# Products of zeros on TensorE ahead of the first useful work, with a newly searched order of all engines

## The chip, the cores and the metric

The kernel runs on one core of one Trainium2 chip. The metric is the device time of one execution in microseconds (us); lower is better. Most executions of a kernel agree within half a percent, so the differences here (0.3 to 1.2%) need several executions each. Two single executions fell in a slow state (311.9 us at a granted clock of 0.951, and 308.81 us); they are left out of the ratios.

A ratio is the mean time of one kernel's fast executions over that of the kernel before, in the same rounds on the same chip. It comes with a 95% interval, and it is not quite the ratio of the medians quoted beside it.

Engine names: PE is TensorE, PEld its weight loads, DVE is VectorE, ACT is ScalarE, POOL is GpSimd, SP is SyncE.

## The reference

Sliding-window attention with a linear bias, followed by a two-layer network whose activation is h·cos(h).

```python
B, H, S, D = 8, 8, 576, 64; window = 128; d_ff = 2048
scores = q @ k.T / sqrt(D) + bias, only where 0 <= row - col < window
attn   = softmax(scores) @ v
x = attn.transpose(0, 2, 1, 3).reshape(4608, 512)
h = x @ w_in                      # 512 -> 2048
out = (h * cos(h)) @ w_out        # 2048 -> 512
```

## The kernel before

The program is a list of operations with their reads and writes. A packed table (`STARTS`) gives each a place on a common time line, in units of 25 ns. The operations are sorted by it and each engine's queue is filled in that order. Waits are derived from the reads and writes. So the table changes only the order; how long a wait lasts is decided on the chip.

```python
def load_v(b, order=range(NBLK)):
    for t in order:
        op("pool", [lambda e, ...: e.dma_start(vp[b % 2][0:rows, t, :, 0:64], v[b, ...])],
           r=[("vinit", b % 2)], w=[("v", b % 2, t)], dma=f"ldv{b % 2}{t}", ...)

def constants():
    for i in range(2):
        op("dve", lambda e, i=i: e.memset(vp[i][:, :, :, 64:65], 1.0), w=[("vinit", i)])
        op("dve", lambda e, i=i: e.memset(vp[i][64:128, 4, :, 0:64], 0.0), w=[("vinit", i)])
        op("dve", lambda e, i=i: e.memset(Pt[i][:, 1024:1088], 0.0), w=[("Pt", i)])
    # ... cos bias, tails of the key tiles

load_first_q()                    # SP issues it, ACT and DVE cast it
load_qk("k", k, 0, 0)             # POOL from here: first keys
distances(); identity()           # POOL computes
load_qk("q", q, 0, 1); load_qk("k", k, 0, 1)
constants()
load_v(0, range(2))               # waits for the clearing of vp[0] on DVE
load_w_in(0); load_v(0, range(2, NBLK))
masks()
for n in range(2):
    qk_transposes(0, "q", n, 0, OB); qk_transposes(0, "k", n, 0, UB)
for u in range(1, 4): load_w_in(u)
load_qk("q", q, 1); load_qk("k", k, 1)
for u in range(4): load_w_out(u)
load_v(1)
```

After that come scores, exponentials, masks, products with V, and nine stages of the network; the network's first stage (stage 0) starts while attention of the first batch still runs.

The softmax here doesn't subtract the row's maximum and nothing guards it: scores larger than these inputs give would overflow.

Of the kernel before, what the change touches and what calls it, by code (L numbers as in the profile page):

```python
# [14 lines left out]
B, H, S, D = 8, 8, 576, 64  # L15
# [12 lines left out]


STARTS = (  # L30
    "c-oy-4RjM#7S8lXpQEnNCmz~Ifbcpkbr@<5Lz`xjG@)q-w5Ao0r7czF)LKhHt!yi7Es9Wf6}niJgZv#9q#}wUi@TMj3cD+N2"
    "+E&|g1D>fuIs@cJm61hX`1YvN!q4O6)`=Xd2@f>y!+kn-a7^^6f%T=K`s<bi0_I^=m|f9JZRv8unb%D+4cVtxOl_40Y&&094"
    "rWF*HF}Ba9|_t-fQ5rzc|B%{%wQ(tI%c3hSOfY?{Id#15t!}An;IBm|9eQ&wWvbxDXeG$sk?i*QH$oyn*95U8}jA8wxVK_@{"
    "qxmheu|GOl+>O7vXz?-tN(2BkF^wT`{&S}xkgzzqNp90Eq@N8n8C)^G6vt~300u7?|P@EDE-hYI3*FKNOJm2im{hDs7HM!m1"
    "Me;-a?bB5mGA^1^%Vr>S;6v=uhwhjh!Vi0uNEe<qsfoR{54q6b3=7K>lUhbmdvQfO^;w4QYZ6MldD2j1cbjP3=ib2s3V`GTH"
    "Y_QD`R)n~SasZ_SL$_XGA&pMjNqV9nijV6GFT#F_ojPFgL9Q$OKJHQ_H4GX*!(=F6kfFd(8`L>Wk^;lXdiysCL~Z!vc9+r`e"
    ")7H1r|zrY_`m?%iGe`4#x)h{>WjXQl3Ztk<`C?H#-s5%aQS8ZGw_YHkLX?y!{SIx!xOSk!u=#6dt**KY+37d8|*LGctd|f(c"
    "6zsNG<|UTyHRHhq&IZNa6PU0+I!OLE*;o;L5J3m|`*eg@wz-;sn7PdLqPuf(-V1T@0JX1uh?hxZX>~#|4My${=EP$7~-QJPu"
    "$k2V*!9g$FlyzQzs$PM^9LhrIXaOu0*^Id+#}B%Lt_48(jA#IAc|zz7XHE&D=@?Wn<iNq-aJf<sOj8YXeU{+1c(-uk(M!^9a"
    "J2A|@Qp#*DMnki|F_1*t;W$^d6j(Bdo*X#6pjc3f8HYQaDM^tcUE4WARAOGFF8<U+*r_}}*(0jcHOUpm(k@9AgdGo971-?C%"  # L40
    "6Gl&_*SPaaUvTHsaoLVN`0g=n6Goc;JF4(tj!QU>r;Xk>t3ZDBKDA>(HZCLwWzp!b`G{WiCfl0&o(=Pen9<Y9VOGea48&K@D"
    "MExIi^L}td_^%&vv_j<ePyt~M(lCePso%IL`jlzLY5Gvh#2ixBOVhZV48Cs+aV&J%0}fCq*7arK-bw1$_N}ZyYq-gNI*84GZ"
    "Q=oDk9Uf<9VbaB1%ch9M}U<ej!y}q?pJxh!)#NEkF2y<GQ7HzrXI*FZ`<GkbhCLd&Y`vLesk!?w?Ur>0fkLebb4_!f{eW-=;"
    "N9?M0|4mwYZ?PvdAw>FKrp{Cv_WTs`4DwF*ytU6w<H6oUq0!%_cyRn=DcC)yrY7cv18R_boULWz}N!EByV!U!qEguqD{(UdP"
    "!2O}zBq|`!W8fPgqFJ>8T2a(zwYls&UFZtft1%^y{1{|0&u2jfsQ5LYLWu{zML-y{shdyi~nf7G_%O2NE8J9|~CrM2;%Uwj6"
    "Y634o^CCXk0gw@rUiO{9h&1slLPVxKAz_lP<e`>NjjfBvPLd0R_bUAd=yKXIkrWB+k@i3M7i5!M#^mWYXDZo5NgbWOqWI=)A"
    "~XcGFn3rg)fX&VGcDE(xx3P*C4%p}B%R~Us2)ju5|VsAN>AaQgjeh93`ji>S>kERW~}L(31JeCjXWBE+i5T%ni)aHT0uhpbG"
    "6I0mar^C;?d*AY5zC^_?eW)WDTGYX(TQ7j;vjnw=ZgGBIT}GE6Yzim5(W5Q<Pr=h_$&-K?aW4*J2-G%Dvcu9m>chgrzGhJg`"
    "sx9e&YhvM;M+lF2^OC%Dt>d8;fbMkk$o8`~qz6ptAHE?QFdSC>CH73!eD_}Bcq%?r<dct<Yq#brE3{jz%1@>{bthEM~Q%+n{"
    "+hv@U!vM?UsM3Q%jmS;;^<vS;We#??$pLl=k{nK(@U90YGtFdNoJACq@k4lvGAw|!bkx<NZzz_gRlJ`Mb^g)Vv#+ypZ;nAuK"  # L50
    "jJj&<cA|S9m(s#^lRA7FUIIZD9`ezgg^Io?=LvOc7`iQ*iD2Jn1VX0Uw-XJ;7cjvs%6-JdHYl%Ed7M?s6Axi0Q+f#l?PGvby"
    "8QrHI+ahEEHKv!<^g#kki6ZVr|01SU~I~No+V(Gn_L1CSKd0ywVzjwo`kdTc}Awl)5ob_+~(}6&abLm+<sF=^XsXOshxR5_~"
    "BPl*6$kUooTq2ypi<0sa~|q?i6V1L_*1h`cp05T5r8^xB7bPy7%^5pS$MX0mg-CmyQG`F#Xv`t%OhBt^-AM$~d&9VV*}3U!y"
    "-0{gQkS?Pn<x8kuv}$Zx{WP*s2$zpXYUg%CF+!a{7o)?&H7?&0h%JrjsGDX$O;O%3x?lovHO@My_ds(NKP4Fv?{=BkyXnb>?"
    "u%Ew@Xrz0Ti9A4CtB%1A8i0**Xa}(h-$cZUat|Ov{U{JdrW;zS_H06&3l1K?MDepj|)XvJ3?UctV{4?b(QpcdYWtRII^jX*s"
    "nOu2z<qyZ8$r>#y*6o$O*H+EWeZ0<Dwm(qof4BJUQ|q%wh}YAxB*hH~(?h%FW&@qqx9&aXJ>@Mt{t-}Ro~8BJv=#@F5taGyJ"
    "9+vIT-yPdKE#u|2jNf281rInVTs75^C<Z@k#+S$RxL9b<IV<jHUsaFM4eK_wz5StAYW(?ox*!hQ&pu$Ms=KHL^dfC1aqlLaZ"
    "#hQCFjv<Qa?u7{Ph_!U%9<Fy%stfCM8hBl*p3($+kwk*gjFxnn8+clTAhI7m}0a&96e2W3EIG7ECjz)xp~S8kPX%vUQfpg?Q"
    "#Ib!(ba-Fr4X(*C!arE@D@wrp7}%hP+RE4SZ-dx~?Cg!u18%k|f6YJV^XD*T<&E5y<TZ>0MhG(tXh?nG7GvDMa>Hr?>@R%+A"
    "RT7-vVcvLKfnFrEB>CUMUl(f!eWRy=j?HuTByvC*Ed-Ti^B<hBhwf8(#AK@WFww;-n?7U@eg-?e*!{;PyrHs5&*A{A%Bu6Vp"  # L60
    "(cVk7!Yyd+I_b$h>~tUhOu1ELPWII@m^iYsMV};36iaxu{V*1=nA-rwD!5#vq@+r@McXGY9{^>p&`u4fS)~}TEZFEBpINYMN"
    "_*9_RcD&oH@Cl8Mh>k}zI;wt=J`DgztlIsU2~Vksy1g2E=5Ecl8jV~pTQ^x!K9;lc<@JgC^?w-d-el3z*ydaq)jl-`LW&5q!"
    "{53QK>{iRfsQ|GXi-QW{D2$19qu4pwrA<!g3;J^1kIZW1-YeguI*tN)EBS8yRu7%$e)JewNd*fryp%KR2~NbxdL&=`Q8KN!7"
    "-bJ67%Rn3R7rI$yF+v&lZDoR>VZ=k~wg`I1Tb0LvSk4L1<E(W<O(q^nHIldD8WtzuPQ%KXMMZ}mrFO9FgllwyGba|KpaCon`"
    "EAfl3wPywZOBcJv?Vv~3(QrUxOrqAOL>l}niZeE7Yjz_K40>soqeE>lT&x&%~G~BUxF$+Kt(6}6r1MorG6x2zCr{)xY+vsai"
    "CYF4^gf+aisu_m+`y1qAyBdn{ZuPVESE?1nWPir!-&?NayG>-HGMl=0o0J|u{j%cI2N>Hp|E(=0OXfp!*@{*7qSRBX#q<aEw"
    "UOOf_RVAmq<NlNv-`AVx9KQMUjb6)$#Nj=5MN7saTePIRQ*KSSquf<G@JF<njmZS=%1S~<W~E}_?%To`s+5?h>Z}+zida<CP"
    "^wqG>$dD4H-urDatcRS_d{V$3{rI7THy)XH(K3WC^0)3DIhuIF$NB>i+?MBOA>"
)


# [150 lines left out]
def bass_alibi_sliding__then__act_gcu_kernel(  # L222
# [8 lines left out]
    with ExitStack() as ctx:  # L231
# [3 lines left out]
        R = Plan(nc, ctx)  # L235
        op = R.op
# [165 lines left out]
        def tail_zero(b):  # L402
# [3 lines left out]
                    :, 4, :, 64:128], 0.0), w=[("tr", "k", b % 2), ("ktail", b % 2)], occ=250,  # L406
               lat=300)

        def masks():
            for h in range(H):  # L410
                op("act", lambda e, h=h: e.activation(
                    EM[:, h, :], dif[:, :, :].rearrange("p a b -> p (a b)"),
                    ACTF.Exp, scale=slopes[h]), r=["dif"], w=[("EM", h)], occ=306, lat=400,
                   table=0)


        def qk_transposes(b, which, n, part, banks):

            t0, R, groups = PIECES[b][n]
            jj = groups[2 * part:2 * part + 2]  # L420
            c0 = 64 * (t0 // 32)

            def dst(i):
                return ps[:, banks[i], :].bitcast(BF16)[:, 0:128 * (jj[i][1] - jj[i][0])]

            def f(e):
                ins = None
                for i, (j0, j1) in enumerate(jj):
                    for j in range(j0, j1):
# [34 lines left out]
        def scores(us, slot):  # L464
# [577 lines left out]
```

## Time and profile before

| | before |
|---|---|
| median of three executions | 308.57 us |
| span of the profiled one | 306.7 us |
| PE busy | 293.7 us, 96% |
| first work on PE | 5.64 us |
| PE at half speed, by the spacing of its products | 5.64 to 21.44 us |

Busy time and the chain of waits, from the page of the kernel before. The first line is busy time, share of the span and number of instructions of each engine; the second is the chain of waits by engine.

```profile
PE 293.7 (96%) x2881; PEld 198.9 (65%) x2900; DVE 253.0 (82%) x540; ACT 204.6 (67%) x294; POOL 95.2 (31%) x122
PE 93%; DVE 3%; DMA 1%; issue 1%; ACT 1%; ACTq 0%
```

Everything here points at PE. But a matmul's recorded length can be longer than the distance to the next one: at 21.1 us the products of 65 columns are recorded at 0.25 us each and start 0.055 us apart. So an engine can read as 100% busy (PE here 2.98 of the 2.98 us from 18.39 to 21.37 us) while the products stand further apart than they need to.

PE's timeline of the kernel before, in the opening. Columns: start, length of the group, engine and line, operation, output<-inputs, shape, count, and in brackets the idle time before it and what ended it.

```profile
5.64 1.06 PE L431 MATMUL ps<-ident,qrows 128*64 128x128 bf16 x16 [5.64 <-ACT qrows L321]
8.85 0.82 PE L484 MATMUL ps<-qt,kt 64*128 64x256 bf16 x8 [1.29 <-DVE kt L398]
13.69 0.33 PE L569 MATMUL ps<-vp,p 128*128 128x65 bf16 x3 [0.73 <-issue]
18.39 0.42 PE L738 MATMUL ps<-xT,w_inb 128*128 128x256 bf16 x1
19.50 1.67 PE L738 MATMUL ps<-xT,w_inb 128*128 128x256 bf16 x7
23.13 1.26 PE L738 MATMUL ps<-xT,w_inb 128*128 128x256 bf16 x10
26.88 4.20 PE L738 MATMUL ps<-xT,w_inb 128*128 128x256 bf16 x37
```

Seven products take 1.67 us at 19.5 us, 37 take 4.20 us at 26.9 us; in the chain of waits they are 0.23 us and 0.109 us apart. The products of 65 columns stand 0.054 us apart up to 21.4 us and 0.031 us after it. So in this trace the array runs at about half speed at first. The clock record in the trace has its first entry, 1.00, at 21.44 us. Views that print the granted clock assume 1.00 ahead of the first entry (they print 1.00 for 5.64 to 13.69 us and for 13.69 to 21.44 us), and so hide the slow opening, 15.8 us here.

### The profile page before, as it was taken

Reading aid. Unit: us, or ns where it says so; the run is one execution under the profiler, and the core shown is the slowest. Engines: PE = TensorE matmul, PEld = TensorE weight load, DVE = VectorE, ACT = ScalarE, POOL = GpSimd, SP = SyncE. Lnnn points to the kernel's source line nnn. Section 1 sums busy time; section 2 is a strip of 40 time slices with the busy share of each in tenths; the row PEclk is TensorE's granted clock in tenths of the full one; section 3 lists DMA queues with packets and bytes.
Section 4 is the critical chain, followed back from the end, with each engine's and each line's share of the span. In section 5 each row is a group of like instructions: output and inputs, shape, how many; then the busy total and the mean of one; then the engine's idle time right before and its main releaser. Section 6 shows DMA issues by size and latency. Waiting matters only on the chain.

```text
span 306.7 us, 7126 instructions
## 1 busy us (share of the span) xinstructions
PE 293.7 (96%) x2881; PEld 198.9 (65%) x2900; DVE 253.0 (82%) x540; ACT 204.6 (67%) x294; POOL 95.2 (31%) x122
## 2 busy tenths in 40 slices
PE   2799999999999999999999999999999999999995
PEld 2568845545875578546788887468745765566784
DVE  1678885979978998889998998798999976795983
ACT  5796777688585776788765875678747846545311
POOL 5999240007997801770169004000000000000000
PEclk9999999999999999999999999999999999999999
DMA  7999999959999999999699988673033022020223
GB/s 144 142 192 211 207 173 183 111 96 182 176 156 172 158 156 180 164 165 175 100 168 134 191 122 62 113 141 100 18 98 79 0 84 63 2 68 0 71 87 122
DMA packets 148353, 38.09 MB, mean 124 GB/s; under 512 B 133984, under 2 KB 147040, under 8 KB 148320
## 3 DMA queue, kind: packets, MB, share of 16 engines
q0 software_dynamic: 99344, 18.10, 75.0%
q1 hardware_dynamic: 48976, 19.54, 31.2%
q8 instruction: 23, 0.38, 0.5%
q14 instruction: 10, 0.08, 0.1%
HBM read 36.70 MB, written 9.44 MB: 150 GB/s over the span
## 4 chain that ended last, share of the span: by engine, by line
PE 93%; DVE 3%; DMA 1%; issue 1%; ACT 1%; ACTq 0%
PE ps L714 35%; PE ps L855 33%; PE ps L484 5%; PE ps L738 5%; PE ps L799 5%; PE ps L569 3%; PE ps L431 2%; PE ps L572 2%; DMA ob<-in_q_dram 1%; PE ps L676 1%; PE ps L475 1%; PE ps L558 1%; PE ps L556 1%; DVE xnat L610 1%; DVE gT L724 0%
## 5 line engine op out<-in xcount | busy, mean ns | idle before, releaser
L714 PE MATMUL ps<-xT,w_inb 128*128 128x512 bf16 (+1 forms) x557 | 126.2, 355 | 0.9 <-ACT p L514 0.4
L720 ACT ACTIVATE cos<-ps,halfpi 128x512 f32<-128x512 f32 x128 | 82.5, 687 | 47.8 <-PE ps L714 33.8
L724 DVE TENSOR_TENSOR gT<-ps,cos 128x512 f16<-128x512 f32 x128 | 83.1, 686 | 15.6 <-ACT cos L720 14.9
L714 PEld LDWEIGHTS ps<-xT,w_inb 128*128 128x128 bf16 x576 | 54.4, 98 | 44.2 <-DVE gT L724 5.5
L514 ACT ACTIVATE p<-ps 128x768 bf16<-128x768 f32 (+1 forms) x64 | 56.1, 915 | 13.8 <-PE ps L484 9.8
L328 POOL DMA_DIRECT2D vp<-in_v_dram x40 | 33.9, 873 | 65.8 <-PE ps L572 34.5
L538 DVE TENSOR_TENSOR p<-p,emask 128x512 bf16<-128x512 bf16 (+2 forms) x96 | 42.2, 460 | 5.3 <-ACT p L514 5.0
L855 PE MATMUL ps<-wsum,gT 128*128 128x256 f16 x256 | 46.0, 273 | 0.3 <-issue 0.2
L855 PE MATMUL ps<-wsum,gsum 128*128 128x256 f16 x256 | 45.6, 273 | 0.0
L855 PE MATMUL ps<-w_outb,gT 128*128 128x256 f16 x256 | 43.4, 273 | 0.2
L338 POOL DMA_DIRECT2D qnat<-in_q_dram x30 | 25.4, 885 | 24.0 <-DMA qt<-qnat 22.1
L855 PEld LDWEIGHTS ps<-w_outb,gT 128*128 128x128 f16 x256 | 24.8, 98 | 7.0 <-DVE ob L879 0.4
L855 PEld LDWEIGHTS ps<-wsum,gT 128*128 128x128 f16 x256 | 23.8, 98 | 6.3 <-issue 0.3
L855 PEld LDWEIGHTS ps<-wsum,gsum 128*128 128x128 f16 x256 | 23.9, 98 | 6.1 <-issue 0.6
L855 PE MATMUL ps<-w_outb,gsum 128*128 128x256 f16 x128 | 27.6, 273 | 0.2
L338 POOL DMA_DIRECT2D knat<-in_k_dram x30 | 25.5, 906 | 3.8 <-DMA kt<-knat 2.2
L610 DVE TENSOR_TENSOR xnat<-ps,rec 128x256 bf16<-128x256 f32 x56 | 22.2, 418 | 1.0 <-DVE rec L608 0.2
L484 PE MATMUL ps<-qt,kt 64*128 64x128 bf16 (+1 forms) x320 | 20.1, 252 | 1.4 <-DVE kt L398 1.3
L569 PEld LDWEIGHTS ps<-vp,p 128*128 128x128 bf16 x256 | 16.1, 100 | 6.0 <-issue 3.1
L569 PE MATMUL ps<-vp,p 128*128 128x65 bf16 x256 | 19.0, 197 | 0.9 <-issue 0.7
L484 PEld LDWEIGHTS ps<-qt,kt 64*128 64x128 bf16 x320 | 11.7, 98 | 9.6 <-issue 3.8
L572 PE MATMUL ps<-vp,p 128*128 128x65 bf16 x192 | 17.7, 196 | 0.0
(76 smaller groups left out, 335.2 us busy)
## 6 DMA issues: line engine op xcount, KB each, us to landing
out_dram<-ob SPq DMA_DIRECT2D x32, 256.0 KB, 2.7
vp<-in_v_dram POOLq DMA_DIRECT2D x32, 128.0 KB, 7.1
qnat<-in_q_dram POOLq DMA_DIRECT2D x24, 128.0 KB, 8.5
knat<-in_k_dram POOLq DMA_DIRECT2D x24, 128.0 KB, 12.7
w_inb<-in_moe_w_in_dram POOLq DMA_DIRECT2D x4, 512.0 KB, 9.5
w_outb<-in_moe_w_out_dram POOLq DMA_DIRECT2D x4, 512.0 KB, 21.3
out_dram<-ob SPq DMA_DIRECT2D x8, 128.0 KB, 1.8
qrows<-in_q_dram POOLq DMA_DIRECT2D x1, 576.0 KB, 14.7
```

The source lines that it names most:

```text
L328: op("pool", [lambda e, t=t, rows=rows: e.dma_start(vp[b % 2][0:rows, t, :, 0:64], v[b, :, 128 * t:128 * t + rows, :].rearrange("h p d -> ...
L338: fns.append(lambda e, t=t, rows=rows: e.dma_start(nat[which][b % 2][0:rows, t, :, :], src[b, :, 128 * t:128 * t + rows, :].rearrange("h p ...
L484: ins = e.matmul(ps[:, banks[x], c0:c1], keys_ap(b, x, pr, kc), query_ap(b, x, pr, qb, 128 * nb), start=True, stop=True)
L514: op("act", lambda e: e.activation(P[i][:, :, 0:hi], src_[:, :, 0:hi], ACTF.Exp, scale=0.125), w=held + [("P", i)], occ=920 if G else 691, ...
L538: op("dve", lambda e, p=p, m=m: e.tensor_tensor(p, p, m, ALU.mult), r=[("P", i), ("EM", h0), ("EM", h1)], w=[("P", i)] if n != 1 else [("P ...
L569: ins = e.matmul(o, P[i][:, x, d0:d0 + 128], V[:, kc, h, 0:65], start=True, stop=not two)
L572: ins = e.matmul(o, P[i][:, x, p0:p0 + 128], V[:, kc - 1, h, 0:65], start=False, stop=True)
L610: op("dve", lambda e: e.tensor_tensor(o, U[:, :, :, 0:64], rv[:, :, :, None].broadcast_to([128, 2, 2, 64]), ALU.mult), r=[("rec", n % 2)], ...
L714: op("pe", lambda e, kc=kc, c0=c0: e.matmul(ps[:, bank, c0:c0 + n], w_in[:, kc, 128 * fc:128 * fc + 128], xT[:, kc, (r0 + c0) % XR:(r0 + c ...
L720: op("act", lambda e: e.activation(cosb[ci][:, :], ps[:, bank, :], ACTF.Sin, bias=halfpi[:, 0:1]), r=["halfpi"], w=[("B", bank), ("cos", c ...
L724: op("dve", lambda e: e.tensor_tensor(gT[gi][:, fc, :], ps[:, bank, :], cosb[ci][:, :], ALU.mult), r=[("cos", ci)], w=[("B", bank), ("g", ...
L855: op("pe", lambda e, t=t, fc=fc, bk=bk: e.matmul(ps[:, bk, 256 * t:256 * t + 256], lhs(fc, t), rhs(fc), start=first and fc == 0 and (last ...
```

## The change

The intent: in the trace above TensorE is at half speed until 21.44 us, and it idles while the first queries load (until 5.64 us). I expected it to speed up sooner if it is kept busy; no trace had shown that by then. So it is given products of zeros to do, nine of 512 columns at the start and two of 384 before the first scores. Then the order of all engines was searched again.

```diff
 STARTS = (
-    ... the old order, packed
+    ... the new order, packed (every engine's order differs)
 )
+        def warm(count, n, key):
+            if key == "warm":
+                op("dve", lambda e: e.memset(P[NP - 1][:, 0, :], 0.0), w=[("P", NP - 1)], ...)
+            for _ in range(count):
+                op("pe", lambda e: e.matmul(ps[:, SB[3], 0:n], P[NP - 1][:, 0, 0:128],
+                                            P[NP - 1][:, 0, 0:n], start=True, stop=True),
+                   r=[("P", NP - 1)] + (["kfirst"] if key == "warm2" else []),
+                   w=[("B", SB[3]), key], ...)
...
         load_first_q()
+        warm(9, 512, "warm")
         load_qk("k", k, 0, 0)
...
             qk_transposes(0, "k", n, 0, UB)
+            if n == 0:
+                warm(2, 384, "warm2")
```

(Three more lines make the first transposes and the first scores follow the zeros.)

More of the change, by code (lines that the diff above doesn't have):

```diff
@@ L30 @@
 STARTS = (
-    "c-oy-4RjM#7S8lXpQEnNCmz~Ifbcpkbr@<5Lz`xjG@)q-w5Ao0r7czF)LKhHt!yi7Es9Wf6}niJgZv#9q#}wUi@TMj3cD+N2"
-    "+E&|g1D>fuIs@cJm61hX`1YvN!q4O6)`=Xd2@f>y!+kn-a7^^6f%T=K`s<bi0_I^=m|f9JZRv8unb%D+4cVtxOl_40Y&&094"
-    "rWF*HF}Ba9|_t-fQ5rzc|B%{%wQ(tI%c3hSOfY?{Id#15t!}An;IBm|9eQ&wWvbxDXeG$sk?i*QH$oyn*95U8}jA8wxVK_@{"
-    "qxmheu|GOl+>O7vXz?-tN(2BkF^wT`{&S}xkgzzqNp90Eq@N8n8C)^G6vt~300u7?|P@EDE-hYI3*FKNOJm2im{hDs7HM!m1"
-    "Me;-a?bB5mGA^1^%Vr>S;6v=uhwhjh!Vi0uNEe<qsfoR{54q6b3=7K>lUhbmdvQfO^;w4QYZ6MldD2j1cbjP3=ib2s3V`GTH"
@@ L36 @@
-    "Y_QD`R)n~SasZ_SL$_XGA&pMjNqV9nijV6GFT#F_ojPFgL9Q$OKJHQ_H4GX*!(=F6kfFd(8`L>Wk^;lXdiysCL~Z!vc9+r`e"
-    ")7H1r|zrY_`m?%iGe`4#x)h{>WjXQl3Ztk<`C?H#-s5%aQS8ZGw_YHkLX?y!{SIx!xOSk!u=#6dt**KY+37d8|*LGctd|f(c"
-    "6zsNG<|UTyHRHhq&IZNa6PU0+I!OLE*;o;L5J3m|`*eg@wz-;sn7PdLqPuf(-V1T@0JX1uh?hxZX>~#|4My${=EP$7~-QJPu"
-    "$k2V*!9g$FlyzQzs$PM^9LhrIXaOu0*^Id+#}B%Lt_48(jA#IAc|zz7XHE&D=@?Wn<iNq-aJf<sOj8YXeU{+1c(-uk(M!^9a"
-    "J2A|@Qp#*DMnki|F_1*t;W$^d6j(Bdo*X#6pjc3f8HYQaDM^tcUE4WARAOGFF8<U+*r_}}*(0jcHOUpm(k@9AgdGo971-?C%"
@@ L41 @@
-    "6Gl&_*SPaaUvTHsaoLVN`0g=n6Goc;JF4(tj!QU>r;Xk>t3ZDBKDA>(HZCLwWzp!b`G{WiCfl0&o(=Pen9<Y9VOGea48&K@D"
-    "MExIi^L}td_^%&vv_j<ePyt~M(lCePso%IL`jlzLY5Gvh#2ixBOVhZV48Cs+aV&J%0}fCq*7arK-bw1$_N}ZyYq-gNI*84GZ"
-    "Q=oDk9Uf<9VbaB1%ch9M}U<ej!y}q?pJxh!)#NEkF2y<GQ7HzrXI*FZ`<GkbhCLd&Y`vLesk!?w?Ur>0fkLebb4_!f{eW-=;"
-    "N9?M0|4mwYZ?PvdAw>FKrp{Cv_WTs`4DwF*ytU6w<H6oUq0!%_cyRn=DcC)yrY7cv18R_boULWz}N!EByV!U!qEguqD{(UdP"
-    "!2O}zBq|`!W8fPgqFJ>8T2a(zwYls&UFZtft1%^y{1{|0&u2jfsQ5LYLWu{zML-y{shdyi~nf7G_%O2NE8J9|~CrM2;%Uwj6"
@@ L46 @@
-    "Y634o^CCXk0gw@rUiO{9h&1slLPVxKAz_lP<e`>NjjfBvPLd0R_bUAd=yKXIkrWB+k@i3M7i5!M#^mWYXDZo5NgbWOqWI=)A"
-    "~XcGFn3rg)fX&VGcDE(xx3P*C4%p}B%R~Us2)ju5|VsAN>AaQgjeh93`ji>S>kERW~}L(31JeCjXWBE+i5T%ni)aHT0uhpbG"
-    "6I0mar^C;?d*AY5zC^_?eW)WDTGYX(TQ7j;vjnw=ZgGBIT}GE6Yzim5(W5Q<Pr=h_$&-K?aW4*J2-G%Dvcu9m>chgrzGhJg`"
-    "sx9e&YhvM;M+lF2^OC%Dt>d8;fbMkk$o8`~qz6ptAHE?QFdSC>CH73!eD_}Bcq%?r<dct<Yq#brE3{jz%1@>{bthEM~Q%+n{"
-    "+hv@U!vM?UsM3Q%jmS;;^<vS;We#??$pLl=k{nK(@U90YGtFdNoJACq@k4lvGAw|!bkx<NZzz_gRlJ`Mb^g)Vv#+ypZ;nAuK"
@@ L51 @@
-    "jJj&<cA|S9m(s#^lRA7FUIIZD9`ezgg^Io?=LvOc7`iQ*iD2Jn1VX0Uw-XJ;7cjvs%6-JdHYl%Ed7M?s6Axi0Q+f#l?PGvby"
-    "8QrHI+ahEEHKv!<^g#kki6ZVr|01SU~I~No+V(Gn_L1CSKd0ywVzjwo`kdTc}Awl)5ob_+~(}6&abLm+<sF=^XsXOshxR5_~"
-    "BPl*6$kUooTq2ypi<0sa~|q?i6V1L_*1h`cp05T5r8^xB7bPy7%^5pS$MX0mg-CmyQG`F#Xv`t%OhBt^-AM$~d&9VV*}3U!y"
-    "-0{gQkS?Pn<x8kuv}$Zx{WP*s2$zpXYUg%CF+!a{7o)?&H7?&0h%JrjsGDX$O;O%3x?lovHO@My_ds(NKP4Fv?{=BkyXnb>?"
-    "u%Ew@Xrz0Ti9A4CtB%1A8i0**Xa}(h-$cZUat|Ov{U{JdrW;zS_H06&3l1K?MDepj|)XvJ3?UctV{4?b(QpcdYWtRII^jX*s"
@@ L56 @@
-    "nOu2z<qyZ8$r>#y*6o$O*H+EWeZ0<Dwm(qof4BJUQ|q%wh}YAxB*hH~(?h%FW&@qqx9&aXJ>@Mt{t-}Ro~8BJv=#@F5taGyJ"
-    "9+vIT-yPdKE#u|2jNf281rInVTs75^C<Z@k#+S$RxL9b<IV<jHUsaFM4eK_wz5StAYW(?ox*!hQ&pu$Ms=KHL^dfC1aqlLaZ"
-    "#hQCFjv<Qa?u7{Ph_!U%9<Fy%stfCM8hBl*p3($+kwk*gjFxnn8+clTAhI7m}0a&96e2W3EIG7ECjz)xp~S8kPX%vUQfpg?Q"
-    "#Ib!(ba-Fr4X(*C!arE@D@wrp7}%hP+RE4SZ-dx~?Cg!u18%k|f6YJV^XD*T<&E5y<TZ>0MhG(tXh?nG7GvDMa>Hr?>@R%+A"
-    "RT7-vVcvLKfnFrEB>CUMUl(f!eWRy=j?HuTByvC*Ed-Ti^B<hBhwf8(#AK@WFww;-n?7U@eg-?e*!{;PyrHs5&*A{A%Bu6Vp"
@@ L61 @@
-    "(cVk7!Yyd+I_b$h>~tUhOu1ELPWII@m^iYsMV};36iaxu{V*1=nA-rwD!5#vq@+r@McXGY9{^>p&`u4fS)~}TEZFEBpINYMN"
-    "_*9_RcD&oH@Cl8Mh>k}zI;wt=J`DgztlIsU2~Vksy1g2E=5Ecl8jV~pTQ^x!K9;lc<@JgC^?w-d-el3z*ydaq)jl-`LW&5q!"
-    "{53QK>{iRfsQ|GXi-QW{D2$19qu4pwrA<!g3;J^1kIZW1-YeguI*tN)EBS8yRu7%$e)JewNd*fryp%KR2~NbxdL&=`Q8KN!7"
-    "-bJ67%Rn3R7rI$yF+v&lZDoR>VZ=k~wg`I1Tb0LvSk4L1<E(W<O(q^nHIldD8WtzuPQ%KXMMZ}mrFO9FgllwyGba|KpaCon`"
-    "EAfl3wPywZOBcJv?Vv~3(QrUxOrqAOL>l}niZeE7Yjz_K40>soqeE>lT&x&%~G~BUxF$+Kt(6}6r1MorG6x2zCr{)xY+vsai"
@@ L66 @@
-    "CYF4^gf+aisu_m+`y1qAyBdn{ZuPVESE?1nWPir!-&?NayG>-HGMl=0o0J|u{j%cI2N>Hp|E(=0OXfp!*@{*7qSRBX#q<aEw"
-    "UOOf_RVAmq<NlNv-`AVx9KQMUjb6)$#Nj=5MN7saTePIRQ*KSSquf<G@JF<njmZS=%1S~<W~E}_?%To`s+5?h>Z}+zida<CP"
-    "^wqG>$dD4H-urDatcRS_d{V$3{rI7THy)XH(K3WC^0)3DIhuIF$NB>i+?MBOA>"
+    "c-p;I4^&iD8lM5w+uPIjylD=XA&1L@)!DZ=!DE==&YKwm#u0JCBtYD7mURWuZ3#Cu{8JK=x<ux>u7#<cUH{g))KN}(j+SLb="
+    "&I{6D{HsS&X)FPv&{tL&+K<+U>Fz>t8@09^WNP1-S7VSe&6r+-O*@$J(|9!uhpaVX*8odd>UV%3k|Km<KwSJ)7K1nq9P)@uL"
+    "MRknm(tV{xt&zU!Oy8d|+1#zgn%PBkV-Mg-2{@hOqVA;CeSY+8we<r#3R^(-%g6-xty!7_)ESnr;5xs7Or&$3W9QI>M*DJUF"
@@ new lines @@
+    "6J?Sm~*or4UKn!!HWknQ_6^o4}c9byUh8SdLN7<OL>NWr!*1iFC%kGd8(ZkP5doDeea>(UOJzpw=KJ`p`5x`eMXx@|B(+Hg>"
+    "MIBx#7HZ<FVvo@k7gc-hpx){V5txwxOldEkY-2NYa&WNtixxhZZTs7J@f1UwF&38sI{0VdE%~mMS!YrsG3`JiMzoAgP5nO#k"
+    "(ait$1Pzf<SA%D03nsW1?$Mgip0=kmq8G6CfK}W5-O-5b8qp<8mzvR6ud{G}fL%kD8*O;u8Dj1a8r2R>m|j{!x_!Ovi0+V*&"
+    "Y>977BX#g=eMJ{GP|$!7M@P+|A&x6#OE7I*4H8A^+h~P-P80FGJp^?BZAo<!)X@KY%c{PB0ECojryjShh5(Tgw7FN#)RD%H("
+    "lu~dy##n&LM@X`3}PE9wr;17a{*fb#?b^xL<mmP=lcp+4eoO*gY~2dTzkd5mNR;Gab-g;M)_%fMG1!fd4?o@DR1yjuAr)OKQ"
@@ new lines @@
+    "}}A!={n-qTzi=HP*#`wo7+5H;7e0Jr(c!Y*ZB@Vvt--8V#3K5b`6yb=Dt3E^w_hOy;M@O?gkO4R>cPESlU=x$H{P;S@lYI2t"
+    "Ddc^H^y4`h^$)7~kAHigf?{cxWO;@zz8OO%wzjivEwsiP_hugiz*6faRmFXwn{zy%nn*4_0(Fa%7I;FYtM|3y2H%&S#PM`j4"
+    "aRgoZS2}mDLpqBy5?-Ek$o61k>B?DFv0b_)=_)O#IC|x$tCwtxzb_H#5fac^^-lu)ib7H?dr3eTA&i|Y7Ev=n0x=afA}=47^"
+    "lZF<L~xaLES4aN&(*837-kTJ2zwM!FSLj`b1|5N1JbLdQ;!OKOh7tz(7&=E61EcwZYt!~>K=%}9)xXtv{2;3m6GoLGDScxO5"
+    "{m1;v5NE7LLs~dvoWVp6`9(MC)=Q>hH)9FM484Ul{k#Z{2AY$*iB@tN9(XJ|`vn)_#>cI}L(NB_G5+tIYE?6gtF<%2=WyFG|"
@@ new lines @@
+    "1KbXVFqns9=Hc<G(d4d=YPHTK}o6TKU#OT^Wpl&%!u+eC~FmU>)+MWsZPptlQ)PWrIPDfZB<ISLld*p1I+B_^N6L@#0yJ4>*"
+    "rrw58RxbvwZO6=FzB~n(1vALc-w7!}e*xq9o*5^3V<huX9sQ!W$87WIqJk-S2;bqEm>OEAUiRuE*4aZOB!<RiFiG;FKN)4W*"
+    "9<8Eck~&_bGG&W5o8vua^$$&vGAAFD&3}>C&tIIK&Jt2qHE(a7V-+0<>ymTcYB-gK)r60vxALYyz%vCN<}%BcwSTvmkDRyYv"
+    "mSGjN)M8G!V&-IE+-2Wi04obZ?ayAUKbogL=WjC?ybD1mwSx@ihYphmougoC8AYGm}tGghp1jaOOTw1>hf6XQvz~=EeZUJIL"
+    "+2=F95tKJBURI0>j(zddHK-eNjrr-@J=(3457r!<*SH7~6^*zr$iVRUK5yDp2Dw#Yw7KMMM)TGrF*aO{bU`?rGdgFlCRI5F2"
@@ new lines @@
+    "Hyxev=e-SUj_kXd~Ict0cNXi}?e9-C7{=B5BA64FnSx{W)g8^>~n+(aVCwx*gNEqmMA+mlT>sU+9<a+)H&<4vHfRyN14*O?Q"
+    "5UBzEo_8)TBx(}?-c^kb-i6y;6v-~qsX(yF3M+C!5jujwOArMRg7$wKOg@P~=&=X2bUICb;3*tDx=s*e+8~vk+V!3RVP?3P5"
+    "?>GX2;wu)@9Y`LxLRhZdh>@9tE#;c{(o*WgL%0`3Y+$?LTd&T>`Bet>%VdgAI%ek=U^Dv|?D>v|M64+6BOtMveF_NO$^Hly%"
+    "2Htko4Ot7ouux@P>?bngVazq26RBx<xiQ_+|x@_oGo|%o-F%7$w}M1J;U8@zhgzc**()#IWt9kx;_m{OV1fCH@7yJKjc;Coq"
+    "5GZOIp)8vN{bU_nP+$3bc!=ZuLI@>K0SEWkW@LkW+z=&Hxy=poJ;W%!7pJ!#FS~1D+BuDd(F4=(;%3cr)g8?or^8?0g;=vNO"
@@ new lines @@
+    ";4nTb#lTHAoARJHQ$0wg6TfwcjXq`Eg0Dcbr83RE5glpv#o2u753V~d}{_3U+V$qG!}r|nPg-0YM96YxtA@&t<9l7YP@LX}f"
+    "&pvSpz1{rD@WeWgMqfD@2>0U$yqdy&UAr8KWtnS4|B9~(^ku~zIU=KrPp>RNeVOT{?szP8h(#&jyvjWz0WN)iHwIkE2oE06e"
+    "^DCOSpIG`!`hr+?q`{PP7x}0DJu8;1mnY)!cB3=(Wci*sQ$)S^aqFHl?h3c7c(*r;<GX+MIG3&3BNBlGP$c_Y=|U|D;w{E}C"
+    "4{B`3%4gf>~CT?rGFNh_!5T%Rbr_1z&gPa9r+(*@=qW*Ij1#$3re-Zv9nA_vY|U6ym@lslhy_R4J4>=3QdzmslM#ZL(Mp!t+"
+    "c<3J&wjnM9ez86lmtLE=a~8-$q_z*&0qf_8WdBvT2G7gx*%fS2*aW<s}i98`yh(&*@t%H|L6FDeG5Rb{b0BS2Z7RPH{lZ{dE"
@@ new lines @@
+    "7kN={7as>l>Nxl7eaR-0_TzxD<4_)KM=F}6}NTE_qOPCMiDbUd~4T1&1z-E{5i0W1WZfQL4yY=m<JqQcP!1E_GZAqjBN-IwG"
+    "in;lpPWs;zA(U0@KOsWXM0xtm>$31*GjP<$r908WhTX4(WVi7RhLgc*W5`hXh+FC(5Q)W;XmeqAoyXx8Wrc&I+RxdKv)v1dW"
+    "C69t|jV?fiDlS9gH*o#rs8cAlORSATft$M6WmBru$&^ZlsW*85z!`7a0KbJk!tb1!7n`>?zvMWRc%<y)DkW#l>DMxN=q`_R@"
+    "5A>4iDqSc8x~boUD$W&{6!)m*~qib8LE3VP>^_d$VN>lW~#us+l!Jc6LR+^4v~>8A%r;j#UH&|Ksms7<U)3G&0cL>XuU#+M}"
+    "{7%GQtm%qpf@73uG&)LY1(S;u5M;tuUR`&zPW)&6JhNn>>bDPudAE;Oh&;GR>awuXElCHLitvC#h>hSGALUD^aD1sT*4Wi8;"
@@ L69 @@
+    "&6HpB4;yq;y0EtCPLF~>y{Xf&m!N|6c=*X(yCF~z&-jMH*V+AYW)MC2BQQ=14Sq+CGWEU#TOKUeh`AvS&V^EH2l_$VzRHU%Q"
+    "Xx|6bG<Pztoh#2?~x3U1@hssQlELKZ0er(z+e%4UIFI{+JthWhN){Bx~IG`jU+M0LXm9;CAmBYQxrqS|(MaSQ#MO!J0%-U+8"
+    "RwyW+(YT|usm8$m0b4h)y_HG<EsMp9r}XeCdjTXelI+Jxj`0PrxD1ZM0_vepWVo=AX8*xM?FRL<w{}tW7SoR}QP3$4FqNOGC"
+    "2uVz<P#T0&LVF`E0$?W-mMZ`1Q-|D6`ov0Z=@%b1A(-{faI-!W~6SGl2=h*wWoFigk3LdXlHzP{4p5jbL+V`k#Kav`w69h2G"
+    "mEi$A6&-=+^ju$Nvukga^0"
 )
@@ L407, in tail_zero @@
                lat=300)
+        def warm(count, n, key):
+            if key == "warm":
+                op("dve", lambda e: e.memset(P[NP - 1][:, 0, :], 0.0), w=[("P", NP - 1)], occ=190,
+                   lat=270, pri=0)
+            for _ in range(count):
+                op("pe", lambda e: e.matmul(ps[:, SB[3], 0:n], P[NP - 1][:, 0, 0:128],
+                                            P[NP - 1][:, 0, 0:n], start=True, stop=True),
+                   r=[("P", NP - 1)] + (["kfirst"] if key == "warm2" else []),
+                   w=[("B", SB[3]), key], occ=n * 10 // 24, lat=n * 10 // 24 + 165, pri=0)
         def masks():
@@ L436, in qk_transposes @@
             op("pe", f, r=piece_keys(which, b, n) + ["ident"] + (
-                   [("tr", "k", 0, j) for j in (0, 4)] if n else []), w=[("B", x) for x in banks],
+                   ["warm"] if b == 0 and n == 0 else []) + (
+                   [("tr", "k", 0, j) for j in (0, 4)] if n else []),
+               w=[("B", x) for x in banks] + (["kfirst"] if (b, which, n) == (0, "k", 0) else []),
                occ=58 * num, lat=58 * num + 170,
@@ L491, in scores @@
                 occ += 250 if pr == "t" else 220 if G else 165
+            if us[0] == (0, 0, 0):
+                keys.append("warm2")
             op("pe", f, r=keys, w=held, occ=occ, lat=occ + 165, mode=1, pri=2)
```

## The prediction

> **What bounds the kernel now.** TensorE: the page gives PE 293.7 of 306.7 us busy (96%), and the chain of waits is 93% PE. From 24 us on the stretches show PE 97 to 100% busy, so only the opening and the end have room. The opening loses time in three ways:
>
> 1. PE does nothing until 5.64 us. It waits for the first queries: DMA issued at 0.81, landed at 4.96 us, then a 0.64 us cast on ACT.
> 2. From 5.64 to about 21.4 us PE runs at half speed. The timeline shows 128x256 products 0.23 us apart at 19.6 us, 0.109 apart at 27 us; 16 transposes take 1.08 us at 5.64 us, 0.57 us at 37.9 us. The 128x65 products go from 54 to 31 ns apart at 21.4 us: there the clock rose. The row of granted clock says 1.00 throughout and does not show it. [...]
> 3. Gaps before 18.4 us (1.3 us before the first scores, 0.7 at 13 us) where ACT and DVE hold the chain.
>
> **What the change does.** It removes nothing useful. It adds one clearing of a probability tile (about 0.2 us, on an idle DVE at 1 us), nine 128x512 products of zeros (estimated 0.43 us each, twice the 0.21 us of full-rate 512-wide products: 3.8 us, about 1.4 to 5.3 us) while PE waits for the queries, and two 128x384 ones (0.3 to 0.65 us) inside the 1.3 us wait before the first scores. All sit where PE idles, so their cost on the critical path is near zero. It moves the order of everything.
>
> **Worth on the critical path.** If the clock is up by the first transposes:
> - 5.64 to 8.85 us: the first 16 transposes save 0.5 us, the next some more, and the key tail's clearing moves out of the way: scores start at about 7.7 instead of 8.85 us (-1.1).
> - 8.85 to 18.39 us: PE work would halve, but ACT was 4.1 of 4.8 us busy, then 3.2 of 4.7, DVE 3.2 and 3.8. ACT and DVE become the limit; I allow -0.9.
> - 18.39 to 21.37 us: dense PE, 3.0 us becomes 1.5 (-1.5).
> Sum -3.5 us; afterwards PE is dense and keeps the lead. I take off 0.3 us [...].
>
> Predicted **305.3 us**, range **303.6 to 307.6**. Chances: faster by over 2% 0.05, within 2% 0.93, slower by over 2% 0.02.
>
> **What would show it.** Timeline: zeros from about 1.4 us, the last still 0.43 us apart or already 0.22; first transposes still at about 5.6 us, now 0.57 us per 16; 128x65 products about 30 ns apart from the first; first scores near 7.7 us; first product of w_in near 16 us instead of 18.4; waits on ACT and DVE between 8 and 16 us. Total PE busy time about equal (zeros +3 to 4 us, faster work -6). From 24 us on, the same sequence about 3.5 us earlier.
>
> **What would make it wrong.** [...] ACT could already bind the opening, leaving only the 1.5 us of the dense part. The new order could lose or win about 1 us elsewhere, at the end above all.

The three terms came to -3.5 us (-1.1, -0.9 and -1.5), and 0.3 us was taken off as an allowance: 308.6 less 3.2 us is 305.4, put down as 305.3. That zeros would bring the clock up by the first transposes, on which the three terms rest, was my estimate.

## More of the kernel before

The timelines of DVE and POOL of the kernel before hold two lines that I did not weigh before predicting:

```profile
7.57 0.27 DVE L394 MEMSET vp<- 64x256 uint32 x1
8.14 1.77 POOL L328 DMA_DIRECT2D vp<-in_v_dram  x2 [2.61 <-DVE vp L394]
```

POOL sat idle for 2.61 us until DVE had cleared a corner of the first V tile, and only then issued the loads of V, w_in and w_out. PE felt it: its first product with V, at 13.69 us, came 0.09 us after the second part of V had landed (13.60 us), while the masked probabilities had been ready at 12.89. The view says "issue" for this wait of 0.73 us, as it names no releaser.

## The result and the profile after

The changed kernel took 304.94 us (median of six, 303.93 to 306.28) against 308.44 us, ratio 0.9887 [0.9854, 0.992]: 1.1% faster, which is within the 2% band. The prediction, 305.3 us with a range of 303.6 to 307.6, holds it. Its account of where the time comes from does not hold, as the rest of this document shows.

Busy time of the changed kernel, from its page. PE's total is about the same, 294.8 us:

```profile
PE 294.8 (97%) x2911; PEld 197.5 (65%) x2911; DVE 252.0 (83%) x542; ACT 204.0 (67%) x293; POOL 95.0 (31%) x122
```

PE's timeline of the changed kernel in the opening:

```profile
1.26 4.02 PE L415 MATMUL ps<-p 128*128 128x512 bf16 x9 [1.26 <-DVE p L412]
5.76 1.04 PE L442 MATMUL ps<-ident,qrows 128*64 128x128 bf16 x16 [0.48 <-ACT qrows L321]
6.61 0.63 PE L442 MATMUL ps<-ident,krows 128*64 128x128 bf16 x16
7.17 0.50 PE L415 MATMUL ps<-p 128*128 128x384 bf16 x2
8.90 0.51 PE L497 MATMUL ps<-qt,kt 64*128 64x256 bf16 x8 [1.22 <-DVE kt L460]
18.66 1.04 PE L753 MATMUL ps<-xT,w_inb 128*128 128x256 bf16 x8
```

The zeros run where they were meant to. The first 16 transposes still take 1.04 us, because the clock rises only at 6.63 us; the next 16 take 0.63. From then until 13.46 us PE is fast, yet the first scores start at 8.90 us (before: 8.85) and the first w_in product at 18.66 us (before: 18.39). Neither came earlier; the first product with V did, by 0.65 us (13.04 against 13.69).

The clock fell back once. Stretches of the changed kernel, cut at the entries of its clock record. Columns: stretch, length, busy time of PE, PEld, DVE, ACT, POOL, then granted clock, DMA share and GB/s:

```profile
6.63:13.46 6.83, 3.99 (x90) 2.70 (x86) 5.07 (x13) 5.88 (x10) 6.83 (x9) 1.00 1.49 185
13.46:16.87 3.41, 3.30 (x42) 2.36 (x38) 3.06 (x13) 2.31 (x4) 3.41 (x6) 0.50 1.98 175
16.87:24.40 7.53, 7.12 (x107) 5.81 (x106) 5.88 (x17) 7.50 (x13) 7.53 (x10) 1.00 1.25 209
```

So the granted clock was 1.00 for 6.83 us, then 0.50 for 3.41 us, then 1.00 again; the products of 65 columns stand 0.055 us apart at 14.6 us, in the slow stretch, and 0.030 us apart at 18.4 us. What makes the clock fall and rise is not shown. What this fall cost is not isolated: PE was busy for 3.30 of the 3.41 us at half rate.

What did move is the clearing and the loads behind it. DVE and POOL of the changed kernel:

```profile
5.79 0.27 DVE L394 MEMSET vp<- 64x256 uint32 x1
6.36 1.77 POOL L328 DMA_DIRECT2D vp<-in_v_dram  x2 [0.93 <-DVE vp L394]
```

The loads are issued 1.78 us earlier. I took milestones from the traces: the landing of the last of w_out, the end of the first and of the sixteenth product with the cosine into gT (the sixteenth ends the first half of the network's stage 0), and the end.

| milestone, us | before | after | difference |
|---|---|---|---|
| last of w_out landed | 42.9 | 41.6 | -1.3 |
| first product into gT | 24.44 | 23.04 | -1.40 |
| sixteenth product into gT | 41.53 | 39.64 | -1.89 |
| from there to the end | 265.18 | 263.60 | -1.58 |
| span | 306.70 | 303.24 | -3.46 |

So there are two gains, one in the opening and one after it. The border between them is good to about 0.4 us only: at the sixteenth product the new order has also done 12 products with w_out and the old one 10, and these stand 0.22 us apart. There are three suspects: the clock (zeros), the earlier loads, and the rest of the new order.

### The profile page after: what moved, and what is told of

Its sections match the earlier page's. It is cut to its first block, busy times and chain, and to the rows that moved or that the text cites. A ratio compares the mean times of both kernels' runs of the same rounds, so it can differ in the third digit from the quotient of the medians.

```text
span 303.2 us, 7167 instructions
## 1 busy us (share of the span) xinstructions
PE 294.8 (97%) x2911; PEld 197.5 (65%) x2911; DVE 252.0 (83%) x542; ACT 204.0 (67%) x293; POOL 95.0 (31%) x122
## 4 chain that ended last, share of the span: by engine, by line
PE 93%; ACT 2%; DVE 2%; DMA 1%; issue 1%; DVEq 0%
PE ps L729 36%; PE ps L870 33%; PE ps L497 5%; PE ps L814 5%; PE ps L753 5%; PE ps L584 3%; PE ps L587 2%; ACT p L529 2%; DMA ob<-in_q_dram 1%; PE ps L442 1%; PE ps L691 1%; PE ps L488 1%; PE ps L571 1%; PE ps L573 1%; DVE xnat L625 0%
## 5 line engine op out<-in xcount | busy, mean ns | idle before, releaser
L729 PE MATMUL ps<-xT,w_inb 128*128 128x512 bf16 (+1 forms) x576 | 129.7, 355 | 0.2
L870 PE MATMUL ps<-wsum,gT 128*128 128x256 f16 x256 | 46.8, 273 | 0.0
L870 PE MATMUL ps<-w_outb,gT 128*128 128x256 f16 x256 | 43.7, 273 | 0.0
L870 PE MATMUL ps<-w_outb,gsum 128*128 128x256 f16 x128 | 26.3, 273 | 0.0
L497 PE MATMUL ps<-qt,kt 64*128 64x128 bf16 (+1 forms) x320 | 19.2, 245 | 1.4 <-DVE kt L460 1.2
L584 PE MATMUL ps<-vp,p 128*128 128x65 bf16 x256 | 18.4, 195 | 1.8 <-DVE p L553 1.6
L587 PE MATMUL ps<-vp,p 128*128 128x65 bf16 x192 | 17.3, 194 | 0.0
```

The source lines that it names most:

```text
L497: ins = e.matmul(ps[:, banks[x], c0:c1], keys_ap(b, x, pr, kc), query_ap(b, x, pr, qb, 128 * nb), start=True, stop=True)
L584: ins = e.matmul(o, P[i][:, x, d0:d0 + 128], V[:, kc, h, 0:65], start=True, stop=not two)
L587: ins = e.matmul(o, P[i][:, x, p0:p0 + 128], V[:, kc - 1, h, 0:65], start=False, stop=True)
L729: op("pe", lambda e, kc=kc, c0=c0: e.matmul(ps[:, bank, c0:c0 + n], w_in[:, kc, 128 * fc:128 * fc + 128], xT[:, kc, (r0 + c0) % XR:(r0 + c ...
L870: op("pe", lambda e, t=t, fc=fc, bk=bk: e.matmul(ps[:, bk, 256 * t:256 * t + 256], lhs(fc, t), rhs(fc), start=first and fc == 0 and (last ...
```

## The experiments

Theory "clock": the zeros let PE run fast from the start, and the new order only serves that. Rivals: "loads": the order lets the loads start earlier; "rest": the new order gains later, with no regard to either. Twelve runs were made. Unless said otherwise each had five timed rounds beside the kernel before.

### The changed kernel once more

> The changed kernel unaltered, timed beside the others on the same chip. Every theory expects the ratio 0.9887 again, within its interval 0.985 to 0.992 (304.9 us where the kernel before takes 308.4). [...]

Measured: 305.49 us against 308.19, ratio 0.9907 [0.9881, 0.9934]. Its clock rose at 3.97, fell at 10.79 and rose at 17.62 us, where the first profile has 6.63, 13.46 and 16.87. So these moments are not fixed to the kernel's start.

This profile fell on the slowest of its executions (span 304.7), and it shows why. PE's longest waits, by what ended them (total us, times, longest):

```profile
PE ps L497 <- DMA kt<-knat: 1.5, 1, 1.5
PE ps L415 <- DVE p L412: 1.3, 1, 1.3
```

At about 75 us the scores of the third batch waited 1.5 us for keys that a DMA transposes. The first profile of the same kernel had no such wait. Up to 73 us both executions agreed within 0.1 us; from 77 us on they were 1.4 us apart. So the difference between these two executions comes from one tight transfer, although the clock was at half rate twice as long in this one (6.83 us against 3.41). The other executions have no profile.

### The order without the zeros, and the zeros without the order

```diff
 # e1: after the table is read
+gone = set(self.zeros)
+for o in self.all:
+    o.preds = {d: kind for d, kind in o.preds.items() if d not in gone}
+self.order = sorted((o for o in self.all if o not in gone), key=...)
 # e2: the kernel before with warm() added, and the new operations placed by hand
+for o in self.zeros:
+    o.start = 39 if o.eng == ("dve",) else 41 if "warm" in o.w else 245
```

> The new order of all engines, but the eleven products of zeros and the clearing of their tile are taken out. Theory clock (the gain is the earlier full rate, the order only serves it): no gain, ratio to the kernel before 0.997 to 1.003, the clock's first rise at 17 to 22 us, the first product of w_in after 19 us. Theory order (the new order wins by itself, the zeros do little): ratio 0.988 to 0.991. A split in halves would give about 0.994.

> The old order of all engines with the same eleven products of zeros and their clearing put in front, on PE and DVE alone. Theory clock: ratio to the kernel before 0.989 to 0.992, first rise at 5 to 9 us, and from 24 us on the old sequence 2.5 to 3.5 us earlier. Theory order: ratio 0.998 to 1.002 although the clock rises early.

Measured: the order alone 306.77 us, ratio 0.9951 [0.9929, 0.9974], between what the two theories expected. Its clock rose at 13.28 us, sooner than the 17 to 22 us expected, though no zeros ran. The zeros alone 308.96 us, ratio 1.0033 [1.0008, 1.0057]. With the zeros the clock rose at 6.72 us, much as in the changed kernel (6.63). It was at half rate again from 13.54 to 16.96 us, which gives this profile a mean granted clock of 0.994; the other five have 0.989 to 0.993, so it probably fell back in all six executions. And the kernel got no faster; if anything slower. Theory "clock" as I stated it falls here.

Where did the lead of the fast PE go? With the zeros alone, the first product into gT came 1.11 us earlier than before (23.33 against 24.44), the fourth only 0.23 us (28.46 against 28.69), the sixteenth 0.23. PE's waits in that run, and its timeline at that place:

```profile
PE ps L589 <- DMA vp<-in_v_dram: 2.3, 1, 2.3
PE ps L758 <- DMA w_inb<-in_moe_w_in_dram: 0.8, 1, 0.8
...
22.89 1.26 PE L758 MATMUL ps<-xT,w_inb 128*128 128x256 bf16 x10 [0.78 <-DMA w_inb<-in_moe_w_in_dram]
```

It ran into data that had not landed: V (landed at 13.51 us, first product at 13.60), then the second quarter of w_in (landed at 22.85 us, product at 22.89). In the kernel before, the slower PE left 0.73 us of the wait for V and none for w_in.

### Only the loads earlier

One clearing is moved in the old order; no zeros.

```diff
+moved = {281: 41}                 # place of the clearing of vp[0]'s last rows: 7.0 -> 1.0 us
+for o in self.all:
+    if o.eng == ("dve",) and not o.r and o.start in moved:
+        o.start = moved[o.start]
```

> The kernel before, with nothing but one clearing on DVE moved: that of the last rows of the first V tile, for which POOL waits before it issues the loads of V, w_in and w_out, from 7.6 us to 1.3 us. No zeros, old order otherwise. POOL should issue the loads from about 5.5 us instead of 8.1, and w_in's first quarter should land at about 14.5 us instead of 16.4, the last of w_out at about 40.5 instead of 42.9. Theory loads (the new order wins because it lets the loads start 1.8 us earlier, and the loads run back to back until 42 us): ratio 0.992 to 0.997. Theory clock with PE as the limit: loads are not waited for, ratio 0.999 to 1.002.

> The kernel before with the one clearing moved, once more, because its first profile fell in the slow state. Ratio 0.992 to 0.997 again; 16th product into gT at 39 to 40 us instead of 41.5; from there to the end about 265 us as in the kernel before. The clock rises late, at 13 to 22 us, as nothing warms PE.

Measured: 306.23 us against 308.15, ratio 0.9941 [0.9917, 0.9965], with one execution of six slow, the profiled one. Repeated with three rounds: 305.82 against 308.3, ratio 0.9926 [0.9903, 0.9949]. POOL's timeline of the second run:

```profile
5.43 1.77 POOL L332 DMA_DIRECT2D vp<-in_v_dram  x2
```

The wait of 2.61 us is gone. The last of w_out landed at 40.8 us instead of 42.9, the sixteenth product into gT ended at 38.93 instead of 41.53, and from there to the end it took 265.24 us (before: 265.18). So the whole gain is made in the opening. One moved instruction gives 0.6 to 0.7%, more than half of what the whole change gives.

But the clock is not the same in the two profiles: here it rose at 13.43 us, in the kernel before at 21.44, although no zeros run in either. PE's timeline of the second run, at the places shown above for the kernel before (13.69, 18.39 and 23.13 us):

```profile
12.47 0.34 PE L573 MATMUL ps<-vp,p 128*128 128x65 bf16 x3
16.99 0.27 PE L742 MATMUL ps<-xT,w_inb 128*128 128x256 bf16 x1
20.41 1.26 PE L742 MATMUL ps<-xT,w_inb 128*128 128x256 bf16 x10
```

The lead grows from 1.22 to 1.40 and then to 2.72 us, and the last 1.3 us of it came while the kernel before still ran at half rate and this one at full. Early loads with a late rise of the clock were never profiled, so up to half of the 2.6 us may be the clock's, for which the data now were there. Three things speak for the loads all the same. An early clock with late loads (the zeros alone) kept 0.23 us. With almost the same clock record, late loads cost 1.5 us (the changed kernel with late loads, below). And the nine fast executions of these two runs all took 305.80 to 306.55 us, although the moment of the rise can differ between executions of one kernel (6.63 and 3.97 us in the two profiles of the changed kernel); of these nine it is on record for one only.

The lead is complete by the fourth product into gT (26.09 against 28.69 us), 7 us before any of w_out has landed (33.09 us). So it is V and w_in that count here. The landing of w_out only shows when the last of these loads was through (the DMA moved 204 GB/s on average from 18.39 to 42.9 us in the kernel before), and PE waited for w_out in neither profile up to 45 us.

### Zeros together with early loads, in the old order

Both edits above in the kernel before.

> The old order with the zeros (which alone gave 1.0033) and that one clearing moved to 1.3 us. Theory loads: the zeros alone failed because the faster PE ran into loads that had not landed (2.3 us for V, 0.8 us for the second quarter of w_in); with loads about 2 us earlier those waits go and the zeros pay: ratio 0.988 to 0.994. Rival (the rest of the new order, after 24 us, makes the gain): ratio 0.998 to 1.003.

Measured: 306.22 us, ratio 0.9942 [0.9919, 0.9966]; the clock rose at 4.68 us and did not fall. The ratio is at the edge of what theory "loads" expected, and its reason fails: the zeros add nothing to the 0.9941 and 0.9926 of the early loads alone. The sixteenth product into gT ended at 38.60 us instead of 38.93, so full rate from 4.68 instead of 13.43 us won 0.33 us in the opening, and even that cannot be seen in the time.

### The changed kernel with late loads

The clearings of the first and the second V tile change places on DVE (a third small one, placed at 205, moves up to 196); everything else is as in the changed kernel.

```diff
+moved = {205: 196, 288: 197, 197: 288}
```

(POOL's two V loads, which must follow in the common order, are placed after it; POOL's own order is the same.)

> The changed kernel, in which the clearings of the first and the second V tile have changed places on DVE, so that POOL issues the loads of V and the weights from about 8.1 us again instead of 6.4; zeros and all else as in the changed kernel. Theory loads: about 1.3 us of the gain goes, ratio 0.993 to 0.998 where the changed kernel has 0.9887 to 0.9907, with waits of PE for V and w_in. Theory rest of the order: unchanged, 0.988 to 0.991.

Measured: 306.19 us, ratio 0.994 [0.9915, 0.9966], against 0.9887 and 0.9907 for the changed kernel. POOL:

```profile
8.23 1.76 POOL L334 DMA_DIRECT2D vp<-in_v_dram  x2 [2.73 <-DVE vp L400]
```

The last of w_out landed at 43.7 us and the sixteenth product into gT ended at 41.12 us, 1.5 us later than in the changed kernel's first profile. This is the undoing of the early loads, and it takes away most of the 1.89 us that the opening gained. The clock record is almost the same as in the changed kernel's first profile (rise at 6.78, fall at 13.60, rise at 17.02 us, against 6.63, 13.46 and 16.87), so this step is not the clock's.

### The same without the zeros

> The last corner of the cube of three switches (early loads, zeros, rest of the new order): the new order with late loads and without zeros. If the rest of the order is worth about 1.3 us by itself, as the milestones after stage 0 say, but its opening, made for a warm PE, gives that back on a cold one: ratio 0.998 to 1.002. Rival (the three simply add: the rest of the order has its own gain in any company): 0.994 to 0.997.

Measured: 307.63 us, ratio 0.998 [0.9951, 1.0008], as the first of the two expected, but the interval reaches into the other. This fills the last corner of the cube:

| ratio to the kernel before | no zeros | zeros |
|---|---|---|
| old order, late loads | 1 | 1.0033 |
| old order, early loads | 0.9941, 0.9926 | 0.9942 |
| new order, late loads | 0.998 | 0.994 |
| new order, early loads | 0.9951 | 0.9887, 0.9907 |

Half the width of each interval is 0.002 to 0.003, so a single difference of less than about 0.004 cannot be told from none. What stands out: early loads gain in all four pairs, by 0.003 to 0.009 (the least, in the new order without zeros, is not clear of noise by itself). Zeros gain nothing in the old order, and 0.004 to 0.006 in the new one: that is about half of what the whole change gives.

The milestones do not explain this gain of the zeros. In the profiled executions of the new order without zeros, the sixteenth product into gT ended at 39.86 us (early loads) and 40.82 (late loads), with zeros at 39.64 and 39.56 (early) and 41.12 (late). A hint lies in the six times of this run: 306.19, 306.67 and 306.93, then 308.33, 308.37 and 308.42 us. The profile is of the quicker group. Perhaps the slower group is where the clock happened to rise late, and zeros take those out; no profile of that group exists, so this is argued and not shown.

### Grafts: which part of the new order gains

Both tables in one kernel. All operations placed before ACT's third table change (about 40 us) take one order, the rest the other.

```diff
+code = old[o]
+if code >> 1 < 1620: o.start = code >> 1          # with zeros and the early clearing
+else: o.start = 10000 + (new[o] >> 1)             # e12; e13 the other way round
```

> A graft: the old order up to the change of ACT's table at about 40 us, with the zeros and the early clearing (as in the run that gave 0.9942), then the new order to the end. If the new order gains about 1.3 us after stage 0 whatever came before: ratio 0.988 to 0.991, gain in the second part of the trace, 16th product into gT at about 38.6 us as in that run. Rival (the new order after 40 us is no better, the two openings differ): 0.993 to 0.996.

> The other graft: the changed kernel with its zeros up to about 40 us, then the old order to the end. If the gain of the later part is lost: ratio 0.993 to 0.996, 16th product into gT at about 39.6 us. Rival (the opening makes all of the gain): 0.988 to 0.991.

Measured: the old opening (zeros, early loads) with the new rest 305.02 us, ratio 0.9895 [0.9871, 0.992], four executions. The new opening with the old rest 305.5 us, ratio 0.9925 [0.9895, 0.9955]; one of its six times was 307.54, the others 304.96 to 305.81.

The first says it clearly: the same old opening followed by the old rest had 0.9942, so the new rest gives 0.0047, or 1.4 us. In the traces, the time from the sixteenth product into gT to the end was 264.31 us with the new rest and 265.73 with the old. The second graft is between what the two theories expected: 264.79 us for its later part, and an interval that holds both answers.

Over all fast profiles the later part took 265.2 to 265.7 us in the four of the old order, and 264.8 with the old rest grafted on. With the new rest, and the waits for transposed keys (at 73 to 75 us, in one run at 120 us too) taken off, it took 263.4 to 263.8 us, and 264.3 in the graft. Where the openings are the same, and so the border too, that is 1.4 us (old opening) and 1.0 to 1.4 us (new opening). So the new order gains 1.0 to 1.4 us after the opening, and in some executions loses up to 1.5 us of it to that wait. What in the new order makes this gain was not looked into.

### Attempts to get more

More zeros in PE's two waits (five of 384 columns before the first scores, five of 512 before the first products with V), and four clearings that stood on DVE around the first two copies moved to about 1.5 us. (The zeros are read from a gT tile here, so that they can run later.)

```diff
-warm(2, 384, "warm2")
+warm(5, 384, "warm2"); later warm(5, 512, "warm3") into the bank OB[1]
+o.start = 60 (or 61) for the clearings placed at 205, 280, 284 and 288
```

> The changed kernel with two things mended that its trace shows: (1) more products of zeros in its two long waits (five of 384 columns instead of two before the first scores, five of 512 before the first products of probabilities and values), [...]; (2) four clearings that stand on DVE between the first two copies and hold the first scores by about 0.5 us are done at 1.5 us, when DVE is idle. Theory clock expects no fall of the clock and 0.5 to 1.2 us less than the changed kernel, ratio to the kernel before 0.984 to 0.987, first scores at about 8.4 us instead of 8.9. Rival: ACT and DVE bind the opening, so neither matters: ratio as the changed kernel's, 0.989.

Then the first V tile's clearing at 1.3 us in addition, so that loads are issued from 5.4 us:

> The changed kernel with more zeros in its two waits and the early clearings (which together gave 0.9883), and with the first V tile cleared at 1.3 us too, so that the loads are issued from 5.5 us instead of 6.4. Theory loads: 0.5 to 0.9 us less again, ratio 0.984 to 0.987. Rival: the loads are no longer what binds, or the key transposes of the third batch at 74 us take the lead back: ratio as before, 0.987 to 0.990.

Measured: 304.32 us, ratio 0.9883 [0.9858, 0.9907], and 304.88 us, ratio 0.9893 [0.9866, 0.9919], with one slow execution left out. The clock rose at 6.73 and 5.19 us and did not fall in either profile. The first scores of the former came at 8.30 us instead of 8.90. PE's timeline of the former, the second line being the five zeros before the products with V:

```profile
8.30 0.51 PE L508 MATMUL ps<-qt,kt 64*128 64x256 bf16 x8
11.24 1.25 PE L424 MATMUL ps<-gT 128*128 128x512 f16 x5
```

The opening did get shorter: the sixteenth product into gT ended at 39.24 and 38.78 us. But neither time can be told from the changed kernel's two (0.9887 and 0.9907). Waits on DMA came back in the place of what was removed: in the former 1.1 us in all for the transposed keys, and 0.5 us for V; in the latter 1.1 us for the second load of keys, which lands at 10.6 us. No kernel run here clearly beats the changed one.

## Why the prediction was right or wrong

The number was right, 305.3 us predicted and 304.94 measured, but by luck: the steps behind it are mostly not what happened.

- **What bounds the kernel: the step that failed.** I took PE's 96% for the limit and wrote that "only the opening and the end have room", and that ACT and DVE hold the chain in the gaps of the opening. In the opening the loads of V and w_in held PE. The 0.7 us gap at 13 us was the wait for V. Zeros with late loads waited 2.3 us for V and 0.8 us for w_in and kept 0.23 us; late loads in the changed kernel, with almost the same clock, cost 1.5 us. After the opening, too, PE's busy share hid room: the new order gained 1.0 to 1.4 us there.
- **"All sit where PE idles, so their cost on the critical path is near zero."** Mostly right: PE did them between 1.26 and 5.28 us, and at 7.17 us. The clock rose at 3.97 us (the changed kernel once more) to 6.78 us (with late loads) in the profiles with zeros, and at 13.28 us (the order alone) to 21.44 us (the kernel before) without.
- **5.64 to 8.85 us (-1.1).** Wrong. The first scores started at 8.90 us. The first transposes still ran at half speed (and 16 of them take 1.04 us at half and 0.63 us at full rate, so 0.4 us was to be had, not 0.5), and the new order put three clearings on DVE between the copies of queries and keys. Moving them, with more zeros, brought the scores to 8.30 us, but no time that can be told apart.
- **8.85 to 18.39 us (-0.9).** Wrong. The first w_in product came at 18.66 us, not 16.
- **18.39 to 21.37 us (-1.5).** Right in size, but not by the zeros. From the first w_in product to the first product into gT the changed kernel took 4.38 us instead of 6.05; the new order without zeros took 4.37, at full rate since 13.28 us, and the old order with zeros 5.42, with a wait of 0.78 us for w_in in it.
- **Sum -3.5 us by the clock.** The zeros alone won 1.11 us up to the first product into gT, and gave back 0.9 us by the fourth, waiting for w_in. With early loads in the old order they were worth 0.33 us in the opening, not 3.5.
- **"From 24 us on, the same sequence about 3.5 us earlier."** Wrong: 1.4 us earlier at the first product into gT, 1.9 at the sixteenth, and the other 1.6 us were gained after that by the new order (some 0.4 us of this is only work that the new order had done before the border).
- **The 0.3 us taken off, for executions in which the rise comes late.** The moment did differ (6.63 and 3.97 us in the changed kernel's two profiles), but the rise came by 6.78 us in all seven profiles with zeros outside the grafts. In four of them the clock fell again for 3.4 or 6.8 us; in the 3.41 us before the fall PE had been busy for 1.12 to 1.79 us. What makes it rise is not settled: in the kernel before PE was busy for 3.26 of the 3.42 us up to 18.03 us, and the clock rose only at 21.44; in the changed kernel once more it was busy for 2.71 of the 3.41 us up to 3.97 us, and there the clock rose. No effect of the fall on the time shows: of the changed kernel's twelve executions, the four whose mean granted clock is 0.999 or 1.0 took 303.93 to 306.28 us, the seven at 0.994 (the value of the first profile, with its 3.41 us at 0.50) 304.82 to 306.19.

So two errors cancelled: a gain of 3.5 us from the clock that is not there by itself, and gains that I had not counted, about 1.5 us from earlier loads and 1.0 to 1.4 us from the later order. Two things stay open: why the zeros gain 1.2 to 2 us in the new order and nothing in the old, and how much of the early loads' gain comes by way of a clock that rises sooner.

## What to carry to other kernels

An engine that reads 96% busy need not be the limit: ask when the data land, and what holds back the queue that loads them; here a 0.27 us clearing, placed late on an engine that had been idle (for 3.67 us, up to 4.96 us), held back V and all weights by 2.6 us. Here the zeros did not pay while the operands of the useful products had not landed (ratio 1.0033), so mend the loads first; in the old order they did not pay after that either (0.9942, against 0.9941 and 0.9926 without). When a change adds work and also brings a new order, run the order without the work and the work without the order before believing either.
